# Routing's rows and logits by matmuls of 160 columns with the tokens as weights, and other steps of the passes around them

## The chip, the cores and the metric

The kernel runs on one core of a Trainium2 chip. The core has five engines with a queue each: TensorE (PE; its weight loads are shown as PEld), VectorE (DVE), ScalarE (ACT), GpSimd (POOL) and SyncE (SP), which here only issues DMAs. The metric is device time in microseconds; before, three runs took 3408.95 to 3414.18, median 3413.23.

## The reference

Three layers follow each other on 4 x 3072 tokens of width 256.

```python
# 1 attention: z has 64 columns, S = 3072
out = u * (np.maximum(z @ z.T / S, 0) ** 2 @ v)
# 2 mixture of 8 experts on x = out, each token to one expert
logits = x @ w_gate
e_idx = argmax(logits)                     # first of equal ones
gate = softmax(logits)[e_idx] * sigmoid(x @ w_output_gate)[e_idx]
x = gate * (maximum(x @ w1[e_idx], 0) @ w2[e_idx])
# 3 gMLP: u, v = halves of maximum(x @ w_in, 0); v normalised per token
y = (u * (w_spatial @ v_n + b_spatial)) @ w_out
```

All of it is float32. The kernel writes each operand as a high part of type fp32r and a remainder, and sums three fp32r products (high-high, high-low, low-high).

## The kernel before

**Attention** runs over 4 batches, 6 column blocks of 512 tokens (a pass) and 24 row blocks of 128 (steps): `for i, (b, j, k)` in `attention`. A step issues two score matmuls (L263, L264), then the relu, square and split on ScalarE and VectorE (L266 to L275), and, three steps behind (`LAG`), six matmuls with `v` into two PSUM banks (L225 to L227), banks 3 and 4 in even passes, 5 and 6 in odd ones. So a step is 8 matmuls of 512 columns.

**Side work** is written as generators; every `yield` ends a stage, and `pump` advances the first generator of a queue by one stage. The queues are `fore` (routing of the block just finished, one stage a step), `back` (loads and splits of the next batch's z and v, later the experts' weights, `w_prep`) and `slow` (`fill_slots`, then `first_sums`). TensorE, ScalarE, VectorE and SyncE execute in exactly the order in which this code issues; GpSimd's instructions and DMAs are put in order by the build's planner, from its own estimate of when each is ready. A waiting instruction holds up everything behind it on its engine.

**Routing** (`route`, 24 times) multiplies the accumulated banks with `u` (xT, features by tokens), splits xT into xh and xl, and multiplies them with the gate weights as stationary operand `WG` (L337, 4 matmuls of 512 columns into bank 7). The 32 rows of logits are copied (L340), turned to tokens by rows with 4 small transposes (L343), and added up (L347, L348). xT itself is turned in two halves of 4 transposes (L356), each copied to `xtok` (L361). VectorE finds the expert, two rank matmuls (L408, L409) count the tokens per expert, VectorE computes each token's slot (L413 to L421), and four indirect DMAs (L423) scatter the rows of `xtok` (256 features, token number, gate) to `x_slots` in DRAM. `x_slots` has first been filled with zero rows by `fill_slots` (L150, L152), 512 rows a DMA from the two `rows` buffers, which `xtok` uses too.

**first_sums** loads pairs of tiles of the spatial weights into `raw4` buffers (three in all, shared with the preparation of z, v and weights), adds and subtracts on VectorE (L780 to L789, four operations for each of 36 pairs) and stores the results by GpSimd DMAs (L781 to L790); an item takes 5 pumps. In the passes after the first, `slow` is pumped at even steps of passes j = 1, 3, 4, and in the last batch at every step of j = 1 and at even steps of j = 0 and 5.

**End of attention.** In the last pass (b = 3, j = 5) `fore` is pumped twice a step, and after step 12 `first_chunk` issues the loads of the first expert's first 1024 rows (L558), then waits 10 stages and turns the rows by transposes (L569, `moe_x`). The routing of the last block itself runs in the first steps of `moe`.

Of the kernel before, what the change touches and what calls it, by code (L numbers as in the profile page):

```python
# [45 lines left out]
W = D + 2  # L46
# [4 lines left out]
def _f(ap):  # L51
    return ap.bitcast(F32)


class _Kernel:
# [56 lines left out]
    def setup(self):  # L112
        self.low = [self.below.tile([P, 1024], F32R, name=f"G{i}") for i in range(16)]
        self.G = deque(self.low[0:12])
        self.Z = deque(self.kept + self.low[12:])
        self.Z.extend(self.big.tile([P, 1024], F32R, name=f"Z{i}") for i in range(6))
        nc, wk = self.nc, self.wk
        self.tri = self.pe.tile([P, P], BF16, name="tri", bufs=1)
        make_upper_triangular(nc, self.tri, val=1.0, diag=False)
        self.ones = self.pe.tile([P, P], BF16, name="ones", bufs=1)  # L120
        nc.gpsimd.memset(self.ones, 1.0)
        self.WG = self.pe.tile([P, 2, P], F32R, name="WG", bufs=1)
        self.desc = wk.tile([P, E], F32, name="desc", bufs=1)
        self.base = wk.tile([P, 5, E], F32, name="base", bufs=1)
        for e in range(E):
            nc.gpsimd.memset(self.desc[:, e : e + 1], float(E - e))
            nc.gpsimd.memset(self.base[:, 0, e : e + 1], float(e * REG))
        self.fz = [self.rows(), self.rows()]
        for fz in self.fz:
            nc.vector.memset(fz, 0.0)  # L130
        self.tokid = wk.tile([P, NT], I32, name="tokid", bufs=1)
        nc.gpsimd.iota(self.tokid, pattern=[[P, NT]], base=0, channel_multiplier=1)

    def gate_weights(self):
        nc, wk = self.nc, self.wk
        wraw = wk.tile([P, 2, 16], F32, name="wraw", bufs=1)
        nc.gpsimd.dma_start(wraw, self.wg.rearrange("(c p) e -> p c e", p=P))
        nc.vector.tensor_copy(self.WG[:, :, 32:P], self.fz[0][:, 0:2, 0:96])
        nc.vector.tensor_copy(self.WG[:, :, 0:16], wraw)
        nc.vector.tensor_tensor(self.WG[:, :, 16:32], wraw, _f(self.WG[:, :, 0:16]), op=ALU.subtract)  # L140

    def fill_slots(self):
        nc = self.nc
        i = 0
        for e in range(E):
            for r0 in range(0, CAP, 512):
                n = min(4, (CAP - r0) // P)
                fz = self.fz[i % 2][:, 0:n, :]
                i += 1
                nc.gpsimd.iota(fz.bitcast(I32)[:, :, D], pattern=[[1, n]], base=N + e * CAP + r0, channel_multiplier=n)  # L150
# [47 lines left out]
    def attention(self):  # L198
# [44 lines left out]
        for i, (b, j, k) in enumerate(steps):  # L243
# [51 lines left out]
        self.drain(self.fore, self.back, self.slow)  # L295
# [3 lines left out]
    def first_chunk(self):  # L299
# [15 lines left out]
    def route(self, b, j, acc, ut):  # L315

        nc, wk = self.nc, self.wk
        R = self.bank[7]
        last = b == B - 1 and j == NJ - 1
        R0, R1 = (self.bank[6] if last else R), R  # L320
# [5 lines left out]
        tt(xT[:, half[1]], acc[1], ut[:, half[1]], op=ALU.mult)  # L326
        nc.scalar.activation(xh[:, half[0]], xT[:, half[0]], AF.Copy)
# [17 lines left out]
        r1 = R[:, 0:P].rearrange("p (i e) -> p i e", i=4)  # L345
        L = wk.tile([P, 4, 16], F32, name="L")
        nc.vector.tensor_copy(L, r1[:, :, 0:16])  # L347
        tt(L, L, r1[:, :, 16:32], op=ALU.add)  # L348
        yield
        xtok = self.rows()  # L350

        def transposes(h, R):
            for i in range(2):
                for d in range(2):
                    t = (2 * h + i) * P
                    nc.tensor.transpose(  # L356
                        R[:, (2 * i + d) * P : (2 * i + d + 1) * P], xT[:, d * 512 + t : d * 512 + t + P], self.ident
                    )

        def tokens(h, R):  # L360
            nc.scalar.activation(xtok[:, 2 * h : 2 * h + 2, 0:D], R.rearrange("p (i d) -> p i d", i=2), AF.Copy)  # L361

        transposes(0, R0)
# [20 lines left out]
        tokens(0, R0)  # L384
# [7 lines left out]
        transposes(1, R1)  # L392
# [7 lines left out]
        tokens(1, R1)  # L400
        ts(eg, eg, 1.0, None, op0=ALU.add)
        nc.vector.reciprocal(eg, eg)
        nc.vector.tensor_copy(xtok.bitcast(I32)[:, :, D], self.tokid[:, col : col + 4])
        tt(xtok[:, :, D + 1], eg, sm, op=ALU.mult)
# [30 lines left out]
    def w_prep(self, e, dst):  # L435
        nc = self.nc
        for q in range(4):
# [9 lines left out]
            yield  # L447
            yield
# [112 lines left out]
    def moe_x(self, rows, nt, dst, into=None, T=None):  # L561
# [22 lines left out]
        nc.vector.tensor_copy(ids[:, 0:nt], rows.bitcast(I32)[:, 0:nt, D])  # L584
        nc.vector.tensor_copy(gate[:, 0:nt], rows[:, 0:nt, D + 1])
# [23 lines left out]
    def overflow(self):  # L609
# [4 lines left out]
        with tc.If(total > 0):  # L614
            for e in range(E):
                left = nc.values_load(tiles[0:1, e : e + 1], min_val=0, max_val=most)
                with tc.If(left > 0):
                    fz = self.rows()
                    nc.gpsimd.memset(fz, 0.0)
                    nc.gpsimd.iota(fz.bitcast(I32)[:, 0:1, D], pattern=[[1, 1]], base=DUMP + e * P, channel_multiplier=1)  # L620
# [10 lines left out]
                    with tc.For_i(0, left, 1) as i:  # L631
# [3 lines left out]
                        for c in range(2):  # L635
                            nc.tensor.transpose(bank[6][:, c * P : (c + 1) * P], rows[:, 0, c * P : (c + 1) * P], self.ident)
# [10 lines left out]
                        for f in range(8):  # L647
# [3 lines left out]
                        nc.vector.tensor_scalar(y[:, 0:D], acc, rows[:, 0, D + 1 : D + 2], None, op0=ALU.mult)  # L651
                        nc.gpsimd.indirect_dma_start(
                            out=self.yt[:, :],
                            out_offset=bass.IndirectOffsetOnAxis(ap=rows.bitcast(I32)[:, 0, D : D + 1], axis=0),
# [4 lines left out]
    def moe(self):  # L659
# [41 lines left out]
        for i, (c, f) in enumerate(seq):  # L701
# [53 lines left out]
            if i >= 8 * 4 + LAG:  # L755
                self.pump(self.slow)
# [642 lines left out]
```

## Time and profile before

| | us |
|---|---|
| median of three runs | 3413.23 |
| profiled execution | 3407.12 |
| its span, first to last instruction | 3405.3 |
| TensorE busy | 3365.8 |
| VectorE busy | 2637.6 |
| ScalarE busy | 1789.9 |
| GpSimd busy | 717.6 |
| mean granted TensorE clock | 0.999 of 2.4 GHz |

Attention takes the span up to about 1130 us, the experts up to about 1750 us, the gMLP the rest. A time of the profile is one execution's. Busy time of TensorE is the union of its instructions; single matmuls overlap, so the distance between two starts is the cost of one, not its duration.

### The profile page before, as it was taken

The page shows a single profiled execution, that of the slowest core. Times are in us where ns is not written, and L with a number is a line of the kernel's source. Part 1 is how long each engine was busy: PE and PEld are TensorE (multiplying, and loading weights), DVE is VectorE, ACT ScalarE, POOL GpSimd, SP SyncE. Part 2 cuts the span into 40 slices and gives each one's busy share as a digit, 9 for nine tenths or more (in the row PEclk, how much of TensorE's full clock was granted, in tenths as well). Part 3 has the DMA queues.
Part 4 walks back from the last instruction along what each step waited for, and adds up shares of the span by engine and source line. Part 5 has one row for each costly group of instructions (what it writes and reads, how often), then busy time and mean ns, then how long its engine had stood idle before and what let it go on. Part 6 is the DMA issues. An engine that isn't in the chain of part 4 may idle for free.

```text
span 3405.3 us, 49613 instructions
## 1 busy us (share of the span) xinstructions
PE 3365.8 (99%) x17616; PEld 3032.1 (89%) x17616; DVE 2637.6 (77%) x4776; ACT 1789.9 (53%) x3118; POOL 717.6 (21%) x1068
## 2 busy tenths in 40 slices
PE   8999999999999999999999999999999999999999
PEld 6888888888877888888888889999999999999999
DVE  7888888888887788877768886576767777877777
ACT  8878878888777433333334453333334333343433
POOL 3121110111212456665533320000000000100000
PEclk9999999999999999999999999999999999999999
DMA  7231232232422578877648887577767576975854
GB/s 268 81 101 50 88 95 77 75 99 85 148 87 91 202 263 273 284 262 255 238 166 298 296 321 264 188 255 238 267 225 270 184 280 213 272 266 185 284 190 165
DMA packets 269413, 676.66 MB, mean 199 GB/s; under 512 B 30256, under 2 KB 118080, under 8 KB 269152
## 3 DMA queue, kind: packets, MB, share of 16 engines
q1 hardware_dynamic: 186144, 408.19, 36.3%
q0 software_dynamic: 83008, 265.18, 21.8%
q8 instruction: 140, 2.29, 0.3%
q14 instruction: 121, 0.99, 0.1%
HBM read 427.68 MB, written 245.57 MB: 198 GB/s over the span
## 4 chain that ended last, share of the span: by engine, by line
PE 62%; DVE 3%; DMA 2%; issue 2%; POOL 1%; ACT 1%; SPq 0%; DVEq 0%; POOLq 0%; ACTq 0%
PE bank L1196 11%; PE bank L1197 11%; PE bank L1198 11%; PE bank L678 4%; PE bank L739 2%; PE bank L740 2%; PE bank L741 2%; PE bank L679 2%; PE bank L963 1%; PE bank L1078 1%; PE bank L961 1%; PE bank L962 1%; PE bank L891 1%; PE bank L890 1%; PE bank L889 1%
## 5 line engine op out<-in xcount | busy, mean ns | idle before, releaser
L275 DVE TENSOR_TENSOR lo<-a,hi 128x512 fp32r<-128x512 f32 x576 | 398.6, 693 | 142.0 <-ACT a L271 79.0
L1309 ACT ACTIVATE wh<-raw 128x768 fp32r<-128x768 f32 x294 | 248.0, 845 | 420.6 <-PE bank L1198 319.4
L226 PE MATMUL bank<-lo,G 128*128 128x512 f32 x1152 | 450.6, 391 | 4.4 <-DVE lo L275 4.4
L225 PE MATMUL bank<-hi,G 128*128 128x512 f32 x1152 | 449.4, 390 | 0.0
L227 PE MATMUL bank<-hi,G 128*128 128x512 f32 x1152 | 449.0, 390 | 0.0
L1310 DVE TENSOR_TENSOR wl<-raw,wh 128x768 fp32r<-128x768 f32 x294 | 281.0, 956 | 210.6 <-ACT wh L1309 209.5
L266 ACT ACTIVATE r<-bank 128x512 f32<-128x512 f32 x576 | 342.6, 595 | 170.0 <-PE bank L264 158.6
L1197 PE MATMUL bank<-wl,R 128*128 128x384 f32 x1288 | 430.3, 334 | 1.2 <-DVE wl L1310 1.2
L1196 PE MATMUL bank<-wh,R 128*128 128x384 f32 x1288 | 430.3, 334 | 0.2 <-ACT os L1088 0.2
L1198 PE MATMUL bank<-wh,R 128*128 128x384 f32 x1288 | 430.2, 334 | 0.0
L268 ACT ACTIVATE hi<-r 128x512 fp32r<-128x512 f32 x576 | 365.2, 634 | 18.3
L1198 PE MATMUL bank<-wh,K 128*128 128x384 f32 x1064 | 355.4, 334 | 0.0
L1196 PE MATMUL bank<-wh,K 128*128 128x384 f32 x1064 | 355.4, 334 | 0.0
L1197 PE MATMUL bank<-wl,K 128*128 128x384 f32 x1064 | 355.4, 334 | 0.0
L743 ACT ACTIVATE hh<-bank 128x512 fp32r<-128x512 f32 (+2 forms) x256 | 132.8, 519 | 377.4 <-PE bank L741 333.3
L273 DVE TENSOR_TENSOR a<-r 128x512 f32<-128x512 f32 x432 | 296.5, 686 | 26.4 <-ACT r L266 26.0
L226 PEld LDWEIGHTS bank<-lo,G 128*128 128x128 f32 x1152 | 216.4, 188 | 54.5 <-DVE lo L275 9.0
L678 PE MATMUL bank<-G,hh 128*128 128x512 f32 x728 | 263.8, 395 | 0.0
L225 PEld LDWEIGHTS bank<-hi,G 128*128 128x128 f32 x1152 | 216.6, 188 | 46.4 <-ACT hi L268 0.4
L227 PEld LDWEIGHTS bank<-hi,G 128*128 128x128 f32 x1152 | 216.5, 188 | 45.2
L745 DVE SCALAR_TENSOR_TENSOR hlo<-bank,hh 128x512 fp32r<-128x512 f32 (+2 forms) x256 | 150.4, 588 | 125.6 <-ACT hh L743 111.0
L1197 PEld LDWEIGHTS bank<-wl,R 128*128 128x128 f32 x1288 | 241.8, 188 | 1.6 <-DVE wl L1310 1.5
(299 smaller groups left out, 7716.7 us busy)
## 6 DMA issues: line engine op xcount, KB each, us to landing
raw<-w_parts SPq DMA_DIRECT2D x240, 384.0 KB
ra<-v_ops SPq DMA_DIRECT2D x147, 512.0 KB
raw<-wsq SPq DMA_DIRECT2D x126, 384.0 KB
v_ops<-vu POOLq DMA_DIRECT2D x84, 512.0 KB
xi<-partial SPq DMA_DIRECT2D x48, 768.0 KB
w_parts<-raw POOLq DMA_DIRECT2D x144, 192.0 KB
u_hid<-vu POOLq DMA_DIRECT2D x48, 512.0 KB
us<-u_hid SPq DMA_DIRECT2D x31, 768.0 KB
```

The lines of the kernel that those rows point to most:

```text
L225: nc.tensor.matmul(acc[d], vh[:, c], hi, start=(k == 0), stop=False)
L226: nc.tensor.matmul(acc[d], vh[:, c], lo, start=False, stop=False)
L227: nc.tensor.matmul(acc[d], vl[:, c], hi, start=False, stop=(k == NK - 1))
L266: nc.scalar.activation(r, sb, AF.Relu, scale=1.0 / S)
L268: nc.scalar.activation(hi, r, AF.Square)
L273: nc.vector.tensor_tensor(a, r, r, op=ALU.mult)
L275: nc.vector.tensor_tensor(lo, a, _f(hi), op=ALU.subtract)
L678: nc.tensor.matmul(acc, hh[:, tc_], w, start=(f == 0), stop=False)
L1196: nc.tensor.matmul(ps, vh, wh[:, ws], start=(k == 0), stop=False)
L1197: nc.tensor.matmul(ps, vh, wl[:, ws], start=False, stop=False)
L1198: nc.tensor.matmul(ps, vl, wh[:, ws], start=False, stop=(k == 5))
L1310: tt(lo, raw, _f(hi), op=ALU.subtract)
```

## The change

A routing's rows and logits now come from one kind of matmul: 128 tokens of xh or xl are the stationary operand, and the moving one is `WG`, 160 columns wide: for feature half 0 the identity and then the 32 gate columns, for half 1 the gate columns and then the identity. Written to columns 0 to 159 and 128 to 287 of a bank, they give 128 features, 32 logit sums, and 128 features. The row in `x_slots` keeps the logits: 290 numbers instead of 258, features of half 1 from column 160. The banks are those of the accumulator just read (6 and 7 for the last routing). The stages' pumps, the filling of the slots, the sums' pace, the weights' preparation and the last pass change too.

```diff
-W = D + 2
+XD = 160
+ID = D + 32
+W = ID + 2
...
-        self.fz = [self.rows(), self.rows()]
+        self.fz = [self.big.tile([P, 2, W], F32, name="fz", bufs=2) for _ in range(2)]
...
-        nc.vector.tensor_copy(self.WG[:, :, 32:P], self.fz[0][:, 0:2, 0:96])
-        nc.vector.tensor_copy(self.WG[:, :, 0:16], wraw)
-        nc.vector.tensor_tensor(self.WG[:, :, 16:32], wraw, _f(self.WG[:, :, 0:16]), op=ALU.subtract)
+        for c in range(2):
+            g = self.WG[:, c, 128 - 128 * c :]
+            nc.vector.tensor_copy(self.WG[:, c, 32 * c : 32 * c + P], self.ident)
+            nc.vector.tensor_copy(g[:, 0:16], wraw[:, c])
+            nc.vector.tensor_tensor(g[:, 16:32], wraw[:, c], _f(g[:, 0:16]), op=ALU.subtract)
...
-            for r0 in range(0, CAP, 512):
-                n = min(4, (CAP - r0) // P)
+            for r0 in range(0, CAP, 256):
+                n = min(2, (CAP - r0) // P)
...
             if b == B - 1 and j == NJ - 1:
-                self.pump(self.fore)
-                if k == 12:
+                if k % 2 or k > 14:
+                    self.pump(self.fore)
+                if k == 14:
                     self.first_chunk()
             self.pump(self.back)
             if i < NK:
                 self.pump(self.back)
-                self.pump(self.slow)
-                self.pump(self.slow)
-            elif b == B - 1 and j == 1 or i % 2 == 0 and (j in (1, 3, 4) or b == B - 1 and j in (0, 5)):
+                for _ in range(3):
+                    self.pump(self.slow)
+            elif i % (2 if j in (1, 3, 4) else 4) == 0:
                 self.pump(self.slow)
...
-        self.drain(self.fore, self.back, self.slow)
+        self.drain(self.fore, self.back)
...
-            for _ in range(10):
+            for _ in range(6):
                 yield
             yield from self.moe_x(self.rows0.pop(0), 4, self.x0, held, self.bank[3:5])
...
-        R0, R1 = (self.bank[6] if last else R), R
+        out = self.bank[6:8] if last else acc
...
         tt(xT[:, half[1]], acc[1], ut[:, half[1]], op=ALU.mult)
+        yield
         nc.scalar.activation(xh[:, half[0]], xT[:, half[0]], AF.Copy)
...
-        yield
-
-        for n, (x, d) in enumerate(((xh, 0), (xh, 1), (xl, 0), (xl, 1))):
-            nc.tensor.matmul(R, self.WG[:, d, :], x[:, half[d]], start=(n == 0), stop=(n == 3))
-        yield
-        lg = wk.tile([32, 512], F32, name="lg", bufs=1)
-        nc.scalar.activation(lg, R[0:32, :], AF.Copy)
-        yield
-        for i in range(4):
-            nc.tensor.transpose(R[:, i * 32 : (i + 1) * 32], lg[:, i * P : (i + 1) * P], self.ident[0:32, 0:32])
...
+        if not last:
+            yield
+        xtok = self.rows()
         L = wk.tile([P, 4, 16], F32, name="L")
+        for h in range(2):
+            for r in range(2):
+                R, i = out[r][:, 0:ID], 2 * h + r
+                for n, (x, d) in enumerate(((xh, 0), (xh, 1), (xl, 0), (xl, 1))):
+                    nc.tensor.matmul(
+                        R[:, P * d : P * d + XD],
+                        x[:, d * 512 + i * P : d * 512 + i * P + P],
+                        self.WG[:, d, :], start=(n == 0), stop=(n == 3), skip_group_check=True,
+                    )
+            yield
+            for r in range(2):
+                nc.scalar.activation(xtok[:, 2 * h + r, 0:ID], out[r][:, 0:ID], AF.Copy)
+            yield
+            if not h and not last:
+                yield
+        tt(L, xtok[:, :, P : P + 16], xtok[:, :, P + 16 : P + 32], op=ALU.add)
+        yield
...
-        transposes(0, R0)
...
-        tokens(0, R0)
...
-        transposes(1, R1)
...
-        tokens(1, R1)
...
@@ def w_prep
-            yield
-            yield
+            for _ in range(2 if e else 4):
+                yield
...
@@ def moe_x
-                nc.tensor.transpose(T[c][:, i * P : (i + 1) * P], rows[:, i, c * P : (c + 1) * P], self.ident)
+                nc.tensor.transpose(T[c][:, i * P : (i + 1) * P], rows[:, i, c * XD : c * XD + P], self.ident)
...
@@ def moe
-            if i >= 8 * 4 + LAG:
+            if i >= 8 or e:
                 self.pump(self.slow)
```

Token number and gate are read at `ID` and `ID + 1` where they stood at `D` and `D + 1`.

## Rows read from the trace of the kernel before

**Rows 1.** The page's part 1, the whole span: engine, busy us (share) x instructions.
```profile
PE 3365.8 (99%) x17616; PEld 3032.1 (89%) x17616; DVE 2637.6 (77%) x4776; ACT 1789.9 (53%) x3118; POOL 717.6 (21%) x1068
```

**Rows 2.** Windows of attention: stretch, length, each engine's busy us, PEclk, DMA, GB/s.
```profile
97.00:141.50 44.50, 44.50 (x205) 36.43 (x204) 35.62 (x76) 41.15 (x74) 4.03 (x6) 1.00 0.25 76
898.00:942.50 44.50, 43.40 (x198) 35.06 (x197) 37.46 (x83) 32.56 (x57) 13.88 (x21) 1.00 0.55 173
942.50:987.00 44.50, 42.80 (x196) 34.73 (x195) 37.21 (x79) 35.44 (x65) 7.28 (x8) 1.00 0.22 69
1076.00:1120.50 44.50, 40.84 (x186) 32.13 (x185) 33.05 (x76) 30.68 (x54) 8.99 (x13) 1.00 0.33 111
10.00:20.00 10.00, 8.95 (x32) 6.93 (x32) 7.79 (x13) 8.62 (x17) 1.37 (x4) 0.83 0.99 355
```

**Rows 3.** Timeline of TensorE, a routing in mid-attention: start us, us, engine, line, op, tiles.
```profile
628.02 0.39 PE L227 MATMUL bank<-hi,G 128*128 128x512 f32 x1
628.34 0.43 PE L343 MATMUL bank<-ident,lg 32*128 32x32 f32 x4
...
629.04 0.40 PE L264 MATMUL bank<-K,K 128*128 128x512 f32 x1
...
636.35 0.39 PE L227 MATMUL bank<-hi,G 128*128 128x512 f32 x1
636.58 0.60 PE L356 MATMUL bank<-ident,e 128*128 128x128 f32 x4
...
637.25 0.39 PE L264 MATMUL bank<-K,K 128*128 128x512 f32 x1
```

**Rows 4.** Timeline of TensorE, a stretch of 256-column matmuls.
```profile
1202.48 0.28 PE L739 MATMUL bank<-e,K 128*128 128x256 f32 x1
1202.60 0.28 PE L740 MATMUL bank<-e,K 128*128 128x256 f32 x1
```

**Rows 5.** Timeline of TensorE's weight loads, behind a routing's rank matmuls.
```profile
640.72 0.19 PEld L263 LDWEIGHTS bank<-K,G 128*128 128x128 f32 x1
640.83 0.19 PEld L264 LDWEIGHTS bank<-K,G 128*128 128x128 f32 x1
```

**Rows 6.** Groups by line, ScalarE, 97 to 850 us: busy us, mean ns | idle.
```profile
L361 ACT ACTIVATE rows<-bank 128x512 f32<-128x512 f32 x32 | 18.6, 582 | 0.0
...
L340 ACT ACTIVATE lg<-bank 32x512 f32<-32x512 f32 x16 | 9.1, 569 | 0.0
```

**Rows 7.** Timeline of TensorE, last pass of attention; in brackets idle and releaser.
```profile
1092.97 0.66 PE L356 MATMUL bank<-ident,e 128*128 128x128 f32 x4 [1.25 <-DVE L L348]
...
1098.87 0.18 PE L408 MATMUL bank<-ohb,tri 128*128 128x32 bf16 x1 [0.45 <-ACT rows L361]
...
1117.14 1.03 PE L569 MATMUL bank<-ident,rows 128*128 128x128 f32 x8
```

**Rows 8.** Timeline of VectorE, GpSimd and SyncE's queue in the same pass.
```profile
1103.48 0.17 DVE L421 CAST slot<-sl 128x4 int32<-128x4 f32 x1
...
1108.82 0.97 POOL L423 DMA_INDIRECT x_slots<-rows,slot  x1 [0.30 <-issue]
...
1111.57 0.33 SPq L558 DMA_DIRECT2D rows<-x_slots  x1
```

**Rows 9.** Timeline of the first two passes: GpSimd, SyncE's queue, VectorE.
```profile
48.35 0.55 POOL L152 DMA_DIRECT2D x_slots<-rows  x1 [0.30 <-POOL rows L150]
...
51.35 0.12 POOL L150 IOTA rows<- 128x4 int32 x1 [0.68 <-DMA x_slots<-rows]
...
76.69 0.55 POOL L781 DMA_DIRECT2D w_parts<-raw  x1
...
79.33 0.54 POOL L790 DMA_DIRECT2D w_parts<-raw  x1
...
81.05 1.43 SPq L776 DMA_DIRECT2D raw<-wsq  x2
...
86.62 0.56 DVE L780 TENSOR_TENSOR raw<-raw 128x384 f32<-128x384 f32 x1
```

More of the change, by code (lines that the diff above doesn't have):

```diff
@@ L121, in setup @@
         nc.gpsimd.memset(self.ones, 1.0)
-        self.WG = self.pe.tile([P, 2, P], F32R, name="WG", bufs=1)
+        self.WG = self.pe.tile([P, 2, XD], F32R, name="WG", bufs=1)
         self.desc = wk.tile([P, E], F32, name="desc", bufs=1)
@@ L145, in fill_slots @@
         for e in range(E):
-            for r0 in range(0, CAP, 512):
-                n = min(4, (CAP - r0) // P)
+            for r0 in range(0, CAP, 256):
+                n = min(2, (CAP - r0) // P)
                 fz = self.fz[i % 2][:, 0:n, :]
                 i += 1
-                nc.gpsimd.iota(fz.bitcast(I32)[:, :, D], pattern=[[1, n]], base=N + e * CAP + r0, channel_multiplier=n)
+                nc.gpsimd.iota(fz.bitcast(I32)[:, :, ID], pattern=[[1, n]], base=N + e * CAP + r0, channel_multiplier=n)
                 dst = self.xs[e * REG + r0 : e * REG + r0 + n * P, :]
@@ L333, in route @@
         yield
-        yield
-        for n, (x, d) in enumerate(((xh, 0), (xh, 1), (xl, 0), (xl, 1))):
-            nc.tensor.matmul(R, self.WG[:, d, :], x[:, half[d]], start=(n == 0), stop=(n == 3))
-        yield
-        lg = wk.tile([32, 512], F32, name="lg", bufs=1)
-        nc.scalar.activation(lg, R[0:32, :], AF.Copy)
-        yield
-        for i in range(4):
-            nc.tensor.transpose(R[:, i * 32 : (i + 1) * 32], lg[:, i * P : (i + 1) * P], self.ident[0:32, 0:32])
-        yield
[L345 to L348, printed above, removed]
-        yield
[L350 to L361, printed above, removed]
-        transposes(0, R0)
+        if not last:
+            yield
+        xtok = self.rows()
+        L = wk.tile([P, 4, 16], F32, name="L")
+        for h in range(2):
[5 more added lines that the diff above has]
+                        x[:, d * 512 + i * P : d * 512 + i * P + P],
+                        self.WG[:, d, :],
+                        start=(n == 0),
+                        stop=(n == 3),
+                        skip_group_check=True,
+                    )
[6 more added lines that the diff above has]
+        tt(L, xtok[:, :, P : P + 16], xtok[:, :, P + 16 : P + 32], op=ALU.add)
+        yield
+        R = self.bank[7]
         col = b * NK + j * 4
@@ L399, in route @@
         yield
-        tokens(1, R1)
         ts(eg, eg, 1.0, None, op0=ALU.add)
         nc.vector.reciprocal(eg, eg)
-        nc.vector.tensor_copy(xtok.bitcast(I32)[:, :, D], self.tokid[:, col : col + 4])
-        tt(xtok[:, :, D + 1], eg, sm, op=ALU.mult)
+        nc.vector.tensor_copy(xtok.bitcast(I32)[:, :, ID], self.tokid[:, col : col + 4])
+        tt(xtok[:, :, ID + 1], eg, sm, op=ALU.mult)
         yield
@@ L583, in moe_x @@
         gate = wk.tile([P, 4], F32, name="gate", bufs=3)
-        nc.vector.tensor_copy(ids[:, 0:nt], rows.bitcast(I32)[:, 0:nt, D])
-        nc.vector.tensor_copy(gate[:, 0:nt], rows[:, 0:nt, D + 1])
+        nc.vector.tensor_copy(ids[:, 0:nt], rows.bitcast(I32)[:, 0:nt, ID])
+        nc.vector.tensor_copy(gate[:, 0:nt], rows[:, 0:nt, ID + 1])
         yield
@@ L619, in overflow @@
                     nc.gpsimd.memset(fz, 0.0)
-                    nc.gpsimd.iota(fz.bitcast(I32)[:, 0:1, D], pattern=[[1, 1]], base=DUMP + e * P, channel_multiplier=1)
+                    nc.gpsimd.iota(fz.bitcast(I32)[:, 0:1, ID], pattern=[[1, 1]], base=DUMP + e * P, channel_multiplier=1)
                     tail = nc.values_load(
@@ L635, in overflow @@
                         for c in range(2):
-                            nc.tensor.transpose(bank[6][:, c * P : (c + 1) * P], rows[:, 0, c * P : (c + 1) * P], self.ident)
+                            nc.tensor.transpose(bank[6][:, c * P : (c + 1) * P], rows[:, 0, c * XD : c * XD + P], self.ident)
                         nc.vector.tensor_copy(x[:, 0 : 2 * P], bank[6][:, 0 : 2 * P])
@@ L650, in overflow @@
                         y = wk.tile([P, 512], F32, name="yo", tag="t2r", bufs=3)
-                        nc.vector.tensor_scalar(y[:, 0:D], acc, rows[:, 0, D + 1 : D + 2], None, op0=ALU.mult)
+                        nc.vector.tensor_scalar(y[:, 0:D], acc, rows[:, 0, ID + 1 : ID + 2], None, op0=ALU.mult)
                         nc.gpsimd.indirect_dma_start(
                             out=self.yt[:, :],
-                            out_offset=bass.IndirectOffsetOnAxis(ap=rows.bitcast(I32)[:, 0, D : D + 1], axis=0),
+                            out_offset=bass.IndirectOffsetOnAxis(ap=rows.bitcast(I32)[:, 0, ID : ID + 1], axis=0),
                             in_=y[:, 0:D],
```

2 lines of the change are left out of this document (removed).

## The prediction

> **What bounds the kernel now.** I read the page's busy times first: TensorE is busy 3365.8 of 3405.3 us [rows 1], so its 39 us of idle time are all that removed waits can give back, and anything larger must come out of TensorE's own work. Then the windows over attention, the only stage in which routing runs: a pass (24 steps, some 46 us) in the undisturbed middle shows TensorE busy 44.50 of 44.50 us while ScalarE has 3.35 us left even in the fullest pass and VectorE 8.9 [rows 2]. So there time follows TensorE's instructions one for one. Three windows have idle TensorE: two in the last batch (1.10 and 1.70 us) and the one that holds the last but one routing (3.66 us) [rows 2]. The reader is to see in the timelines what one routing costs TensorE [rows 3 to 5], and in the last group of chains what its result has to pass through before the experts' first rows arrive [rows 7, 8].
>
> **TensorE's work per routing: the largest term.** Matmuls of 512 columns follow each other every 0.23 us (636.35 to 636.58) [rows 3]. A routing now issues 4 logit matmuls of that kind, 4 x 0.23 = 0.92 us; 4 small transposes, which with the gap ahead of them take 629.04 - 0.23 - 628.25 = 0.56 us (628.25 is where the next matmul would have begun) [rows 3]; and twice 4 transposes of 128 columns, each four 637.25 - 0.23 - 636.58 = 0.44 us [rows 3]. Sum 0.92 + 0.56 + 0.88 = 2.36 us, and all of it goes. The two rank matmuls stay.
>
> In their place come 16 matmuls (4 token tiles x 2 halves of D x high and low part) with the tokens as weights and 160 moving columns. No row shows an fp32r matmul of 160 columns. From below: 256 columns come every 0.12 us [rows 4], 512 every 0.23; on that line 160 cost 0.08. From above: never dearer than the 0.23 of 512 columns. Between them stands the weight load, which each of the 16 needs anew: the closest pair of fp32r loads starts at 640.72 and 640.83, 0.11 us apart [rows 5], and the four 128-column transposes, each with a load, also come to 0.11 each. A matmul cannot start before its weights, and 0.11 is more than 0.08, so I take 0.11: 16 x 0.11 = 1.76 us. Saved 2.36 - 1.76 = 0.60 us per routing, 24 routings, **-14.4 us**; at 0.08 it is 2.36 - 1.28 = 1.08, -26 us; at 0.23 it is 3.68 - 2.36 = 1.32, +32 us.
>
> The Trainium skill has a rule for each side ("TensorE: Matmul & The Clock Gate"). Its section "LDWEIGHTS (loading the stationary operand)" makes a load cost its columns over 1.2 GHz, 107 ns for 128 columns; by that rule the estimate is 16 x 0.107 = 1.71 us, and the trace's 0.11 agrees. Its section "Back-to-back issue gap" gives an isolated matmul its columns over 2.4 GHz plus 2.5 ns, 69 ns for 160; by that rule the saving would be an estimated 30 us. The 256-column row, 0.12 us where that rule gives 0.109, is above it, and no run here shows a narrower fp32r one.
>
> **ScalarE and VectorE.** ScalarE loses the logit copy and two token copies (0.57 + 2 x 0.58 = 1.73 us) [rows 6] and gets four copies of 288 columns. Each costs less than a 512-column copy and more than half of one: 1.2 to 2.3 us. Either end moves it by under 0.6 us per pass, inside its 3.35 us of room [rows 2]; cost zero, cover TensorE. VectorE loses one small copy. The gate weights take six small operations instead of three just before the first step, where TensorE waits for VectorE: **+0.6 us**. The slots' rows grow from 1032 to 1160 bytes; scatters and loads stay as many, and their landing is priced below.
>
> **Waits that go.** In the last batch the sums are now paced evenly instead of at every step of one pass, the first expert's weights get two more steps between load and use, and each routing has free steps between a copy and the matmuls that read it. Of the 1.10 + 1.70 us [rows 2] I take **-2.5** (from none to -4, since a pipelined matmul hides part of a gap). The last but one routing now advances two stages in every step, and TensorE waits for nearly each (one is 1.25 us at 1092.97) [rows 7]; 3.66 us in that window. It will advance two stages in every other step: I take **-3.2** (-5 to -1.5). Late next is the low part of the tokens, made one step ahead of the matmul that reads it: some 0.5 us.
>
> **A wait that comes.** I count pumps through the last pass. Before, the last but one routing's rank matmuls go out at step 9 and the transposes of the first expert rows at step 18: 1098.87 and 1117.14, 18.3 us apart, with no wait at the end [rows 7]. After, the routing has 18 stages, one per even and two per odd step from step 2: rank matmuls at step 13, scatter in the same step, row loads after step 14, and with 6 free steps (two per step) instead of 10 the transposes again at step 18. That leaves 5 steps of 8 matmuls, 5 x 8 x 0.23 = 9.2 us. The chain in between stays: ranks at 1098.87, slots at 1103.48, four scatters on GpSimd's queue whose last starts at 1108.82, the loads on SyncE's queue at 1111.57 [rows 7, 8], 12.7 us. VectorE no longer has sums in the way, -0.8; a load has to land, 3.0 us by a 516 KB transfer (issued 48.35, its buffer free at 51.35) [rows 9]. 12.7 - 0.8 + 3.0 = 14.9, so TensorE stands 14.9 - 9.2, about **+6 us**, at the transposes, with everything behind them in its queue. Bounds: 5 (slots another us earlier) to 9 (18.3 - 9.2). A gap may also lower the clock: in the first stretch, after idle time, 10 us ran at a granted 0.83 [rows 2], 1.7 us lost between the two levels; I take **+1** (0 to 1.7).
>
> **The first pass.** Zero tiles go out as 56 transfers instead of 32, on two buffers of their own. GpSimd's work per transfer is iota, 0.3, issue 0.55: 1.0 us [rows 9]. A 516 KB one holds its buffer 3.0 us, so a pair of buffers gives one per (3.0 + 0.42) / 2 = 1.7 us; 290 KB ones hold it hardly shorter. So 24 more transfers make the filling end later, by up to 24 x 1.7 = 41 us, by some 27 if smaller ones lose less to the other loads. The first sums' stores share GpSimd's queue, in an order that the build's planner chooses by its own times: before, the first (76.69) follows 31 of the 32 fills, the fourth starts at 79.33; it frees the buffer of a load at 81.05, and VectorE uses that at 86.62 [rows 9]. Of these 5.6 us the landing takes 3.0, and VectorE runs some two steps, 4 us, ahead of TensorE: 6.6 us of slack, or four transfers. If the planner again puts a store where its data are ready, it lands among fill 31 to 36 and the delay is nearly eaten by the slack. I take **+3**, from -2 (smaller transfers crowd the first loads less) to +21 (all 56 first: 27 - 6.6). The rest of the sums moves inside GpSimd's and VectorE's free time: no cost, cover TensorE; the 0.55 us operations on VectorE are the same 144.
>
> **Sum.** -14.4 - 2.5 - 3.2 + 0.6 + 6 + 1 + 3 = -9.5 us. The profiled execution is 3405.3 us of span, 3407.1 in all; the runs' median is 3413.2. I take the difference over: 3407.1 - 9.5 = 3397.6 on the profile's footing, **3404 us** on the median's.
>
> **Rivals.**
> A, the weight load hides: the 160-column matmuls come every 0.08 us. For it: the line through 256 and 512 columns. Against: no two fp32r loads are nearer than 0.11. Another 12 us: 3392.
> B, ends on the other side: GpSimd's queue in the first pass. If the fourth store of the sums stands behind more than some 36 fills, VectorE waits at its next sum and TensorE with it; each fill beyond costs 1.7 us, all 56 about 21 instead of the 3. For it: GpSimd already waits for the fills' transfers (0.68 us at 51.35) [rows 9], and the buffer's chain has only 6.6 us to spare. Against: the planner did put a store before the last fill. -9.5 + 18 = +8.5: 3422, and it decides from about 41 fills on (5 x 1.7 = 8.5 us; the saving is gone at 9.5).
> C, narrow fp32r matmuls cost as much as wide ones: +32 for -14.4, that is 3404 + 46 = 3450. For it: no row below 256 columns. Against: 384 and 256 columns both get cheaper in proportion.
> D, the waits only move: the removed 5.7 us stay, the row wait is 9 and the clock falls: about 3414.
>
> **How the numbers follow.** Forecast 0.50 (its own range 3396 to 3412), A 0.15, B 0.17, C 0.08, D 0.10. Range 3386 to 3427: it holds the forecast, D, most of A and B, and leaves out C, A's end (-26 with no row wait) and B's. What tells from no change is 0.2%, 6.8 us: faster means under 3406.4, slower over 3420. Faster: three quarters of the forecast, all of A, 0.53. Slower: C and more than half of B, 0.19. The rest, 0.28, within.
>
> **What would show it.** Right: 16 matmuls per routing 0.11 apart and a pass shorter by 0.6 us; no idle TensorE in the two windows of the last batch; a gap of 5 to 9 us ahead of the first row transposes, released by the row load. Wrong: a spacing of 0.08 or 0.23; a VectorE wait for a sum's load near 86 us with TensorE idle behind it; no gap at the row transposes, which would mean that my count of steps, or the chain's length, is off.

## The result, and the profile after

The changed kernel takes **3441.82 us** (median of six runs, 3438.67 to 3447.12) against 3411.29 of the kernel before in the same session: ratio 1.009, interval [1.008, 1.010], 0.9% slower. The forecast was 3404, its range ended at 3427. The profiled execution has a span of 3439.7 us, 34.4 more than before.

The page's part 1 after (engine, busy us, share, instructions) answers to [rows 1]:

```profile
PE 3370.0 (98%) x17616; PEld 3042.3 (88%) x17616; DVE 2629.3 (76%) x4755; ACT 1778.4 (52%) x3142; POOL 739.0 (21%) x1116
```

TensorE's busy time rose by 4 us, though a pass has less work; part of that work ran at a lower clock (below). The span rose by 34, so 30 us are new idle time. The starts of the rank matmuls mark every pass, and say where the time went:

| stretch (us) | before | after | change |
|---|---|---|---|
| start to the second routing's rank matmuls | 133.1 | 156.3 | +23.3 |
| from there to the last but two routing's, 20 passes | 927.2 | 931.6 | +4.3 |
| from there to the experts' first matmul | 68.6 | 67.1 | -1.5 |
| experts' first to last matmul of layer 1 | 613.2 | 618.7 | +5.5 |
| from there to the end | 1663.2 | 1666.0 | +2.8 |

The experts' matmuls are counted here by those with the weights' low part, the first of which starts 0.5 us after the stage's first. The mark itself has moved: the routing has three stages more ahead of its rank matmuls, which now stand behind the scores of 19 steps of the next pass instead of 16. So 3 x 1.81 = 5.4 of the 23.3 us are the mark's own shift, and the two passes lose 17.8; the third stretch is shorter by the same 5.4, and its -1.5 hides a loss of 3.9.

**An undisturbed pass got shorter, as forecast.** The distance between rank matmuls is 46.13 us before and 45.49 after. The timeline of TensorE around a half routing after (start, duration, engine, line, operation, tiles), as [rows 3]:

```profile
695.38 0.39 PE L231 MATMUL bank<-hi,G 128*128 128x512 f32 x1
695.60 1.02 PE L347 MATMUL bank<-WG,e 128*128 128x160 f32 x8
696.46 0.43 PE L267 MATMUL bank<-K,K 128*128 128x512 f32 x1
```

Eight matmuls of 160 columns take 696.46 - 695.60 = 0.86 us, 0.108 each. "TensorE: Matmul & The Clock Gate" of the Trainium skill, section "LDWEIGHTS (loading the stationary operand)", makes a load take its columns over 1.2 GHz, for 128 columns an estimated 107 ns; the distance of 0.108 us agrees.

**The first two passes lost it again, more than all of it.** Timelines of GpSimd, SyncE's queue and VectorE after (brackets: idle before, and what ended it), as [rows 9]:

```profile
81.20 0.54 POOL L778 DMA_DIRECT2D w_parts<-raw  x1
...
97.12 0.54 POOL L787 DMA_DIRECT2D w_parts<-raw  x1
...
111.81 0.56 POOL L156 DMA_DIRECT2D x_slots<-fz  x1 [0.30 <-POOL fz L154]
...
63.96 51.50 SPq L773 DMA_DIRECT2D raw<-wsq  x4
...
92.34 0.56 DVE L777 TENSOR_TENSOR raw<-raw 128x384 f32<-128x384 f32 x1 [6.51 <-DMA raw<-wsq]
...
118.69 0.56 DVE L777 TENSOR_TENSOR raw<-raw 128x384 f32<-128x384 f32 x1 [9.01 <-DMA raw<-wsq]
```

The four stores of the first item of the sums stand in GpSimd's queue behind 39, 42, 44 and 48 of the 56 fills (before: 31 or 32 of 32); the fourth goes at 97.12 instead of 79.33, the last fill at 111.81. Until a store has gone its load buffer is not free: SyncE needs until 115.46 for four loads, and VectorE stands 6.51 and 9.01 us at the sums' additions, with the low parts that TensorE needs queued behind them. TensorE's two long waits in these passes, and then all its waits from 20 us to the second rank matmuls (total, times, longest):

```profile
94.39 0.50 PE L230 MATMUL bank<-lo,G 128*128 128x512 f32 x1 [4.65 <-DVE lo L279]
119.90 0.79 PE L230 MATMUL bank<-lo,G 128*128 128x512 f32 x1 [5.34 <-DVE lo L279]
```
```profile
PE bank L230 <- DVE lo L279: 11.6, 6, 5.3
PE bank L267 <- ACT r L270: 1.5, 1, 1.5
PE bank L347 <- DVE e L337: 0.7, 1, 0.7
```

Windows after (length, busy us of PE, PEld, DVE, ACT, POOL, then PEclk, DMA share, GB/s), as [rows 2]:

```profile
90.00:100.00 10.00, 5.62 (x19) 4.22 (x20) 7.12 (x20) 4.21 (x9) 3.94 (x11) 0.83 0.62 229
110.00:120.00 10.00, 4.66 (x22) 3.53 (x20) 1.31 (x3) 1.94 (x4) 6.98 (x10) 0.95 0.62 217
120.00:130.00 10.00, 8.02 (x19) 5.35 (x20) 4.83 (x8) 3.78 (x7) 1.24 (x3) 0.67 0.33 107
130.00:140.00 10.00, 9.34 (x40) 7.57 (x39) 8.12 (x14) 9.74 (x19) 0.54 (x1) 0.87 0.41 126
680.00:724.50 44.50, 44.50 (x207) 36.89 (x206) 37.53 (x81) 41.81 (x77) 6.83 (x9) 1.00 0.32 99
1130.00:1140.00 10.00, 3.70 (x17) 2.73 (x15) 4.49 (x8) 3.01 (x6) 4.03 (x4) 0.81 0.38 136
1140.00:1150.00 10.00, 9.69 (x34) 8.08 (x35) 4.21 (x8) 5.10 (x9) 0.00 (x0) 0.68 0.11 45
```

TensorE idles for half of two windows, and the granted clock is 0.67 in the stretch that follows: part of it ran at 1.2 GHz instead of 2.4. In the first four windows the clocks of 0.83, 0.95, 0.67 and 0.87 take 1.7 + 0.5 + 3.3 + 1.3 = 6.8 us, an estimate, beside 13.8 us of idle time. The pass at 680 us has no idle time at all.

**Around the turns from one batch to the next** (and in one pass soon after the first turn) four passes take 4.6, 3.0, 5.7 and 8.4 us more than 45.49, 21.7 in all; before, the same four lose 1.2. The turn at 865 us after, in ScalarE's waits from 852 to 908 us (total, times, longest), and then in the timelines of GpSimd, SyncE's queue and TensorE:

```profile
ACT G L187 <- DMA raw<-v: 11.6, 3, 8.3
```
```profile
863.78 1.12 POOL L420 DMA_INDIRECT x_slots<-rows,slot  x1 [0.30 <-issue]
864.89 0.59 POOL L787 DMA_DIRECT2D w_parts<-raw  x1
...
867.16 7.65 SPq L196 DMA_DIRECT2D raw<-v  x2
...
872.19 0.79 PE L267 MATMUL bank<-G,G 128*128 128x512 f32 x1 [4.92 <-ACT r L270]
```

The last store of an item goes behind a routing's four scatters, the load of v gets the buffer after that, ScalarE waits 8.3 us for it, and the relu behind the split holds TensorE for 4.92.

**The last pass**, timelines of TensorE, VectorE, GpSimd and SyncE's queue after, as [rows 7, 8]:

```profile
1124.33 0.19 PE L405 MATMUL bank<-ohb,tri 128*128 128x32 bf16 x1
...
1128.38 0.17 DVE L418 CAST slot<-sl 128x4 int32<-128x4 f32 x1
...
1133.98 0.97 POOL L420 DMA_INDIRECT x_slots<-rows,slot  x1 [0.30 <-ACT hi L272]
...
1136.85 0.90 SPq L555 DMA_DIRECT2D rows<-x_slots  x2
...
1140.31 1.97 PE L566 MATMUL bank<-ident,rows 128*128 128x128 f32 x8 [6.61 <-DMA rows<-x_slots]
```

Ranks, slots, scatters, loads: the chain and the wait at its end (6.61 us) are those of the prediction.

### The profile page after: what moved, and what is told of

The parts are those of the page before. It is cut to its first block, busy times and chain, and to the rows that moved or that the text cites. A ratio compares the mean times of both kernels' runs of the same rounds, so it can differ in the third digit from the quotient of the medians.

```text
span 3439.7 us, 49756 instructions
## 1 busy us (share of the span) xinstructions
PE 3370.0 (98%) x17616; PEld 3042.3 (88%) x17616; DVE 2629.3 (76%) x4755; ACT 1778.4 (52%) x3142; POOL 739.0 (21%) x1116
## 4 chain that ended last, share of the span: by engine, by line
PE 82%; DMA 7%; DVE 5%; issue 2%; ACT 2%; POOL 1%; SPq 0%; DVEq 0%; POOLq 0%; ACTq 0%
PE bank L1193 11%; PE bank L1194 11%; PE bank L1195 11%; PE bank L230 6%; PE bank L229 6%; PE bank L231 6%; PE bank L675 4%; PE bank L267 3%; PE bank L268 3%; DMA x_slots<-fz 3%; PE bank L736 2%; PE bank L737 2%; PE bank L738 2%; PE bank L676 2%; PE bank L960 1%
```

## The experiments

Where nothing else is said each is the changed kernel with the edit shown and computes everything; ratios are against the kernel before in the same session. "T1" is the start of the second routing's rank matmuls (133.1 before, which is 138.5 at the later place that these matmuls have after; 156.3 after); "turns" the loss of the four passes above; "experts" the time from the first to the last layer 1 matmul (613.2 and 618.7).

### Undoing parts

**The old pace of the sums** (old_pace).
```diff
-            elif i % (2 if j in (1, 3, 4) else 4) == 0:
+            elif b == B - 1 and j == 1 or i % 2 == 0 and (j in (1, 3, 4) or b == B - 1 and j in (0, 5)):
-        self.drain(self.fore, self.back)
+        self.drain(self.fore, self.back, self.slow)
```


> The changed kernel, with the sums' pace of before (pumped only in passes 1, 3, 4 of a batch, all steps of pass 1 in the last one). Theory, sums and preparations share three load buffers: the four TensorE gaps at the turns of passes (4.6, 3.0, 5.7 and 8.4 us over a clean pass of 45.5) vanish, and of some 20 us lost in the first two passes the later half, from 110 to 126 us, goes too; the 4.5 us of the last batch come back: 3442 - 21.7 - 11 + 4.5, about 3414. Rival, the routing's longer chain of stages causes the gaps: they stay, 3440 or more.

3436.34 us, 1.0076 [1.0060, 1.0093]. T1 156.3 as after; turns 8.2 instead of 21.7. So the pace decides most of the turns and nothing of the first passes; the time expected was missed by 22 us: the later half of the first passes' loss, 11 us of my sum, did not go, and 8.2 us stayed at the turns.

**The old fills** (old_fill): 32 of 512 rows from the `rows` buffers, two pumps a step.
```diff
-        self.fz = [self.big.tile([P, 2, W], F32, name="fz", bufs=2) for _ in range(2)]
+        self.fz = [self.rows(), self.rows()]
-            for r0 in range(0, CAP, 256):
-                n = min(2, (CAP - r0) // P)
+            for r0 in range(0, CAP, 512):
+                n = min(4, (CAP - r0) // P)
```


> The changed kernel, with the slots filled as before: 512 rows a transfer, 32 transfers, two pumps a step, from the buffers of the routing's rows. Theory, GpSimd's queue is late by the longer filling and holds the sums' stores, whose buffers the next loads need: the first two passes lose their 20 us, the gaps at the turns of passes stay: about 3422. Rival, the early loss comes from the sums' pace alone: no more than 5 us less, 3437 or more.

3425.21, 1.0044 [1.0029, 1.0058]. T1 149.2: a third of the first passes' loss goes. Part of the rest has another cause here, since xtok now waits for the fills that use its buffers (ScalarE's copies hold TensorE 4.4 us). Turns 21.2.

**Both together** (old_both), and **both with the old last pass** (old_three: `first_chunk` at step 12, two pumps a step, 10 free steps).

> The changed kernel with both the old pace and the old filling. Theory: both losses go and are independent, 3442 - 21.7 - 20 + 4.5, about 3405, with the row wait of 6.6 us before the experts still there; a clean pass stays 45.5 us. Rival, the losses only move elsewhere: 3420 or more.

3423.05, 1.0036 [1.0022, 1.0050].

> As the last one, and the last pass of attention as before: two stages in every step, the first rows' loads after step 12, ten free stages. Theory: the row wait of 6.6 us and the half clock behind it (about 2 us) go, the routing there waits some 3 us at its stages: 3405 - 8.6 + 3, about 3399, 12 below the kernel before, which is the gain of the routing's matmuls (24 x 0.6 us). Rival, the row wait was hidden behind something else: 3405.

3419.59, 1.0024 [1.0014, 1.0034]. Both missed, by 18 and 21 us: T1 stays at 148 to 149, turns at 7, experts at 617 to 619. Undoing the schedule does not give the kernel before with a shorter routing.

### The sums started two passes later (late_sums)

```diff
-            if i == NK:
+            if i == 3 * NK:
                 self.slow.append(self.first_sums())
```


> The changed kernel, with the sums' generator handed in at the start of the fourth pass instead of the second, when the filling is over; pace unchanged. Theory, the first two passes' loss is the sums' stores and loads held up behind the filling in GpSimd's queue: the first passes are clean (some 20 us less) and the gaps at the turns of passes stay: about 3422. Rival, the filling itself or the rows scattered behind it hold TensorE: no more than 8 us less.

3421.31, 1.0034 [1.0021, 1.0046], as expected. T1 136.3, turns 17.7: with no sums in the first passes T1 is 2 us earlier than the 138.5 of before, so the 56 fills alone do no harm that shows.

With the old pace as above, sums also at the end of a batch's first pass, and 13 free steps instead of 6 before the row transposes (late_paced):

> As the last one, with the sums pumped as before (passes 1, 3, 4; in the last batch more) and in the second half of pass 0, and 13 free stages ahead of the first rows' transposes instead of 6. Theory: the first passes, the turns and the row wait are clean but for some 2 us at each of three turns where six value loads follow each other through one buffer: 24 x 0.64 us less than the kernel before, 5 less in its last pass, 6 more at the turns: about 3397. Rival, as in the run with all three parts undone, something of the routing itself costs 20 us: 3412 or more.

3417.67, 1.0027 [1.0017, 1.0036]: missed by 20. The row wait fell to 1.3 us, but the turns stay at 11.9 and the experts at 617, and TensorE waits anew, 6.2 us at 1123 us for a low part: VectorE stands 10.3 us at a sum's addition, whose loads are late, at the end of the last pass.

### What holds the buffers: stores that read something else (const_store)

```diff
-                nc.gpsimd.dma_start(self.parts(n, 5, tb, k), a22)
+                nc.gpsimd.dma_start(self.parts(n, 5, tb, k).rearrange("p (a c) -> p a c", a=3), self.ident.unsqueeze(1).to_broadcast([P, 3, P]))
```
and so for the other three: queues, loads, additions and bytes stay, but the load buffers no longer wait for the stores, nor the stores for VectorE. The sums of the weights are left out of the result.

> The changed kernel, with the stores of the first sums taking their bytes from the identity tile instead of from the load buffers (the weights' sums are left out of the result); as many stores of the same bytes, loads and VectorE operations as before. Theory, a store that waits in GpSimd's queue holds a load buffer, and the next load of values, scores or sums waits for it: with the buffers freed by VectorE alone most of the early 20 us and of the 21.7 us at the turns go, about 3405 to 3412. Rival, the sums' VectorE operations and their loads in SyncE's queue are what delays: 3430 or more.

3410.89, 1.0008 [0.9998, 1.0017]: 31 us less than after, as expected. T1 137.3, turns 8.9. Pace, loads and VectorE's work were as in the changed kernel. The fills were not: the planner put the stores, which depend on nothing now, far ahead among them. GpSimd's timeline, the fourth store and the last fill:

```profile
12.58 0.78 POOL L787 DMA_DIRECT2D w_parts<-ident  x1
...
152.41 0.57 POOL L156 DMA_DIRECT2D x_slots<-fz  x1
```

The fills end 41 us later than after, and still the loss is gone: it was not the fills' end but the hold of the load buffers by the stores. Whether a store holds its buffer because it stands behind fills or because it waits for VectorE this run does not part; the next one does for the first passes.

### The stores on SyncE's queue (sp_store)

```diff
-                nc.gpsimd.dma_start(self.parts(n, 5, tb, k), a22)
+                nc.sync.dma_start(self.parts(n, 5, tb, k), a22)
```
(all four)

> The changed kernel, with the four stores of each item of the weights' sums issued by SP instead of GpSimd; everything is computed. Theory (stores that stand behind fills and scatters in GpSimd's queue hold two of the three load buffers): the first two passes come to 45.5 us each again, the turns between batches lose 2 to 4 us each instead of 3 to 8.4, and the time falls by some 28 to 34 us from 3442, to 3408 to 3415. Rival (the sums themselves, their loads and VectorE's additions at three pumps a step, are the cost, or SP's queue now holds the v and z loads behind the stores): 3425 or more, with ScalarE's wait for v or z at the turns as long as before.

3422.37, 1.0032 [1.0021, 1.0042]: half right. T1 136.7, and TensorE's waits from 20 us up to it fall from 13.8 to 1.0 us. The turns lose 22.3, as much as after, for the rival's reason: v's loads now stand behind stores that wait for VectorE. SyncE's queue in the first passes of this kernel, then ahead of the last turn, and a wait of that queue from 800 to 880 us (total, times, longest):

```profile
77.23 0.32 SPq L787 DMA_DIRECT2D w_parts<-raw  x1
77.65 0.91 SPq L773 DMA_DIRECT2D raw<-wsq  x2
86.35 0.33 SPq L778 DMA_DIRECT2D w_parts<-raw  x1
...
835.96 0.34 SPq L784 DMA_DIRECT2D w_parts<-raw  x1
836.39 0.39 SPq L196 DMA_DIRECT2D raw<-v  x1
```
```profile
SPq L784 <- DVE raw L783: 15.0, 2, 8.4
```

In the first passes the next loads go 0.4 us after the fourth store, while the fills run on to 118.34 us, later than in the changed kernel. "DMA: Bandwidth & Descriptors" of the Trainium skill, section "Issuing engines are not separate DMA queues", says that spreading DMAs over engines saves only the time to issue them. Here it saved more than the issues of 0.54 us each: T1 came 19.6 us earlier, since the stores no longer stood behind fills that wait for their own buffers.

With one more free step between a v quarter's load and its split, and 13 free steps before the row transposes (sp_best):
```diff
         nc.sync.dma_start(raw.rearrange("p (i d) -> p i d", i=4), src)
         yield
+        yield
...
-            for _ in range(6):
+            for _ in range(13):
```


> As the kernel with SP's stores, and two more edits: one more free step between the load of a v quarter and its split, and 13 free steps instead of 6 before the first expert's row transposes; everything is computed. Theory: the 2 to 4 us that are left at each of three turns are ScalarE's waits for v, which land later than one step after their issue, and go (6 us); the row wait of 6.6 us in the last pass falls to about 1 (5 us): 3397 to 3405, below the kernel before. Rival: v comes late because its buffer is late, not because its split comes early, and the transposes that are moved stand on the path at the end of the last pass: 3408 or more.

3407.53, 0.9988 [0.9979, 0.9997], 2.5 us above the range expected. The stretch up to the experts' first matmul went from 67.0 to 59.0 us, more than expected; the turns from 22.3 to 16.9.

### Are the wider rows the experts' 5 us? (wide_rows)

The kernel before with rows of 1160 bytes:
```diff
-W = D + 2
+W = D + 34
...
+        nc.vector.memset(xtok[:, :, D + 2 : W], 0.0)
```


> The kernel before with rows of 1160 bytes instead of 1032 (32 unused columns, set to zero by one more VectorE instruction per routing) and nothing else. Theory: the wider rows are what makes the stage of the experts 3 to 5 us longer in every variant of the changed kernel (608.4 us before, 611 to 613.8 in them), and they lengthen the fills of the first pass: 3414 to 3422, the experts' stage 611 to 613. Rival: the width costs nothing there, the shift has another cause: 3410 to 3413, the experts' stage within 1 us of 608.4.

3411.86, 1.0001 [0.9992, 1.0010]; experts 613.9 for 613.2 (the expectation's 608.4 is the same stage, counted 4.8 us shorter), T1 134.2 for 133.1 (at the place of before). My theory fell: the width costs about 1 us.

### Where the sums can be had

Each of these is the kernel of sp_best with another pace. The first (sp_paced):
```diff
-            elif i % (2 if j in (1, 3, 4) else 4) == 0:
+            elif i % 2 == 0 and j in (1, 3, 4):
```


> The kernel of sp_best (the changed kernel, the sums' stores on SP, one more step before a v quarter is split, 13 free steps before the first expert's row transposes), with one more edit: after the first pass the weights' sums advance at every second step of passes 1, 3 and 4 of a batch alone, not at every fourth of passes 0, 2 and 5 as well; what is left of them runs in the experts' stage. Everything is computed. Theory: at the three turns VectorE and ScalarE have v's split, the routing and the sums at once (VectorE 9.5 of 10 us busy there), and without the sums each turn loses some 2 us instead of 3.8 to 6.0: 8 to 10 us less than 3407.5, 3397 to 3401. Rival: the turn is full without the sums as well, and the sums that are left crowd VectorE in the experts' stage, where TensorE waits for hlo already: 3405 to 3412.

3430.31, 1.0061 [1.0048, 1.0074]. Turns 6.8 instead of 16.9, and attention's end 11.6 us earlier; but 144 pumps do 29 of the 36 items, and the experts take 652 us, which the rival had foreseen, though not its size. The line of the first sums' first addition from 1100 us on (ns least, median, most; first and last start), and TensorE's waits in the whole span of this kernel:

```profile
L778 DVE TENSOR_TENSOR raw<-raw x7: 558/559/559, 1156.5 to 1247.2; 128x384 f32<-128x384 f32 x7
```
```profile
PE bank L737 <- DVE hlo L743: 29.4, 13, 5.5
```

**In the last batch too** (sp_even), where no turn follows: `... or i % 2 == 0 and b == B - 1 and (j or k >= 12)`.

> The kernel of sp_best, but the weights' sums advance after the first pass at every second step of passes 1, 3 and 4 of a batch, and in the last batch, which has no turn behind it, at every second step from the middle of its first pass, so that none is left for the experts' stage. Everything is computed. Theory: the sums at the turns are what is left of the loss in attention (sp_paced showed 47.3 to 48.6 us there instead of 49.3 to 51.5), and the 34 us that sp_paced lost in the experts' stage are the sums that were left over, which crowd VectorE there: 3395 to 3400, the last score matmul near 1107, the experts' stage near 616. Rival: the last batch's passes have no room for the sums either (the kernel before loses 3.4 us in one of them), or w_prep's loads wait for buffers: 3404 to 3410.

3407.92, 0.9999 [0.9990, 1.0008]. I had miscounted: 174 pumps for 180, and two items were still done late (experts 627).

**And in pass 2** (sp_full): `... or i % 4 == 0 and j == 2`, 192 pumps.

> As sp_even, with the weights' sums pumped at every fourth step of pass 2 of a batch too: 192 steps of them in attention, where the 36 items want 180 (sp_even has 174, sp_paced 144, and both ran over: two and seven items were still to be done in the experts' stage). Everything is computed. Theory: attention ends as in sp_even (last score matmul 1105 to 1109), and with nothing left over the first expert's chunks take as long as in sp_best, the experts' stage 616 us instead of 627: 3396 to 3400. Rival: what attention gains is given back at the first expert for another reason, such as w_prep's loads of the next expert's weights, which wait for a G pair: the experts' stage 622 or more, 3404 to 3409.

**3395.98, 0.9969 [0.9959, 0.9980]**, as expected: turns 7.3, experts 615.9, faster than both kernels. So the sums do fit into attention, if they leave the turns free and all end there.

**Three more free steps ahead of the first spatial addition**, in sp_paced, sp_even and sp_full:
```diff
-                yield
-                yield
+                for _ in range(2 if tbs or k else 5):
+                    yield
```


> As sp_paced, with three more free steps between the first loads of the spatial sums and their first addition, which stands ahead of hlo on VectorE and waits 3.9 to 4.5 us for its loads in the variants of the changed kernel (1.64 in the kernel before). Everything is computed. Theory: this wait is what makes the experts' stage 2 to 3.7 us longer at the second chunk of the first expert, and it goes: 2 to 3 us less than sp_paced, the stage from 616 to 613 or 614 us. Rival: the shift has another cause, or the loads move the wait elsewhere: the same as sp_paced within 1 us.

3426.59, 1.0049 [1.0037, 1.0061]: 3.7 us less than sp_paced.

> As sp_even, with three more free steps between the first loads of the spatial sums and their first addition. Everything is computed. Theory: the addition, which stands ahead of hlo on VectorE, waits some 4 us for its loads in every variant of the changed kernel and 1.64 in the kernel before, and this is the 2 to 3.7 us by which the experts' stage grows at the second chunk of the first expert: 2 to 3 us less than sp_even, the stage near 613. Rival: something else holds that chunk (the scatters of y, the weights' loads): within 1 us of sp_even.

3407.37, 0.9997 [0.9988, 1.0006]: 0.6 us less than sp_even, as the rival had it. In both pairs first sums ran over into the experts' stage, so neither settles it.

> As sp_full, with three more free steps between the first loads of the spatial sums and their first addition. Everything is computed. Theory: the wait of that addition for its loads, ahead of hlo on VectorE, is the 2 to 3.7 us by which the second chunk of the first expert comes later: 2 to 3 us less than sp_full, the experts' stage 613 to 614. Rival: something else holds that chunk: within 1 us of sp_full.

**3390.87, 0.9954 [0.9940, 0.9967]**, the fastest. The time fell by more than expected (5 us where 2 to 3 stood, experts 611.3 where 613 to 614 stood), and not by that wait. VectorE's first spatial addition in sp_full, then in sp_full_gap:

```profile
1150.74 0.96 DVE L803 TENSOR_TENSOR sb<-sa,sb 128x768 f32<-128x768 f32 x1 [2.86 <-issue]
```
```profile
1151.80 0.96 DVE L803 TENSOR_TENSOR sb<-sa,sb 128x768 f32<-128x768 f32 x1 [2.80 <-issue]
```

TensorE's waits for hlo in the whole span of sp_full, then of sp_full_gap:

```profile
PE bank L737 <- DVE hlo L743: 4.9, 5, 1.4
```
```profile
PE bank L737 <- DVE hlo L743: 1.9, 4, 0.8
```

The first addition still stands 2.8 us, only behind one more hlo than in sp_full; what fell is the time for which TensorE waits for hlo, 3.0 of the 4.6 us by which the stage got shorter. The three steps move every later spatial sum as well, and only that shift as a whole is what the pair shows.

## Why the prediction was wrong, step by step

- **TensorE's work per routing: right.** 0.64 us a pass saved, 0.60 predicted; 0.108 us a matmul, 0.11 predicted. That is the distance of two weight loads [rows 5], and rivals A (0.08) and C (0.23) fell.
- **Waits that go: right in the last batch**, of whose two slow passes (47.17 and 49.55 us before) the second now takes 45.49, so 3.4 us of waiting went where -2.5 stood; the first is the turn that loses 8.4. The last but one routing's distance fell from 38.55 to 36.42, though 19 steps lie in it instead of 17 (1.81 us each): with the 0.64 us of work taken off, 5.1 us of waiting went, where -3.2 stood with -5 as its bound.
- **The row wait: right**, 6.61 us where +6 stood. **The clock behind it was mis-sized**: PEclk is 0.81 and then 0.68, and the second of these windows alone loses an estimated 3.2 us where +1, at most 1.7, stood. With 13 free steps the wait is 1.3, and the stretch loses 8 us, both terms in one.
- **The first pass: the failing term.** I put +3 and called 31 to 36 fills ahead of the fourth store likely; it was 48. Rival B's own rule, 1.7 us for each fill beyond 36, gives (48 - 36) x 1.7 = 20.4; T1 came at 156.3 where sp_store, with the same fills, has 136.7: 19.6 later. That the two agree so closely is in part luck: of the 19.6 us, 12.8 are idle time of TensorE (13.8 against 1.0) and an estimated 6.8 the lower clock behind it, which the rule did not have. I saw the mechanism and gave it 0.17, arguing that the planner had put a store before the last fill. It did so again, with 48 fills ahead of it. The sign that I had named, VectorE's wait for a sum's load near 86 us with TensorE idle behind it, is the 6.51 us that end at 92.34.
- **"The rest of the sums moves inside GpSimd's and VectorE's free time: no cost": failed.** Another 20.5 us (21.7 at four passes, 1.2 before). I priced the sums by engine time. What they hold is two of three load buffers, for as long as an item lasts, and the passes to which they were spread are those in which z's and v's loads want them. No rival of mine had this; B alone would have ended at 3422.
- **The experts**, where I put nothing, take 5.5 us longer. Row width is not it (wide_rows), nor first sums that run over (none do after). 2.5 of the 5.5 come in the first expert's second chunk (a chunk is up to 512 of an expert's rows), within three steps around VectorE's first spatial addition. Its rows before and then after:

```profile
1165.29 0.96 DVE L805 TENSOR_TENSOR sb<-sa,sb 128x768 f32<-128x768 f32 x1 [1.64 <-DMA sb<-wsq]
```
```profile
1194.64 0.96 DVE L802 TENSOR_TENSOR sb<-sa,sb 128x768 f32<-128x768 f32 x1 [4.29 <-DMA sb<-wsq]
```

It stands ahead of an hlo that TensorE needs, and its loads land later against it. That chunk loses only 0.7 us in sp_full and none in sp_full_gap, whose other gains come later in the stage; so the pair does not show what the 2.5 us were, and why the loads are later is not shown either. The last 2.8 us of the table are open too; the variants, none of which changes that stretch, range there from 1663 to 1668 us.

With the sums away from the turns every variant still loses 6 to 8 us there, the kernel before 1.2. In sp_full the 20 passes of the table's second row lose 9.0 us in all, and these are all of TensorE's waits in them (total, times, longest):

```profile
PE bank L348 <- DVE e L338: 5.0, 4, 1.5
PE bank L231 <- DVE lo L280: 0.8, 2, 0.4
```

The four are the routing's new matmuls, which wait for the low part of the tokens, three of them at the turns. The prediction named this wait, 0.5 us in the last but one routing, and had none at the turns.

## What to carry to other kernels

Price a background job by the buffers it holds and the queue its last instruction stands in, not by the busy time of the engines. A job's last store frees the buffer that the next job's load wants, so a store behind fifty other DMAs is a late load; put it on a queue whose other entries are ready. And price a gap of TensorE with the clock that follows it: here 12.8 us of idle time came with 6.8 us at the lower level. Before spreading a job evenly, look for passes in which something else wants the same buffers, and count that its steps are enough to end where it should.

## What the runs showed that I had not expected

An fp32r matmul of 160 columns with a new 128-column load costs 0.108 us, as much as the 128-column transposes with theirs (0.11 [rows 3]), and 256 columns take 0.12 [rows 4]: from 128 to 160 columns the width was free here. And work left over is dearer than work done in time: 36 pumps, seven items of the sums, cost 36 us in the experts' stage (652.2 against 616.3 in sp_best), about 5 us an item, where sp_full does all 36 items in attention, whose 20 passes behind the first two lose 9 us in all.
